# A fused attention and two-layer MoE kernel: pieces of the weights' conversion queued behind VectorE instructions of the steps

## The chip, the core and the metric

The kernel runs on one core of a Trainium2 chip, as one program. The metric is the device time of one execution in microseconds (us). The numbers of the profile come from one profiled execution, whose records start and end a little inside the device time.

## What is computed

Inputs are float32 queries, keys and values of 8 batches, 8 heads, 576 positions and a head size of 64, and two pairs of float64 weights, which the kernel reads as pairs of 32-bit words.

```python
k_p, v_p = k.reshape(B, H, 72, 8, D).mean(3), v.reshape(B, H, 72, 8, D).mean(3)
attn = softmax(q @ k_p.T / sqrt(D))            # B, H, 576, 72
x = (attn @ v_p) laid out as (4608, 512)
h = x @ w_in;   x = (h * cos(h)) @ w_out        # first layer, w_in 512x2048
h = x @ w_in2;  out = (h * clip(h + 3, 0, 6) / 6) @ w_out2
```

## The kernel before, in words

**Steps.** A layer is worked through in blocks of 512 tokens (9 of them) and in 16 chunks of 128 of the 2048 inner columns. One pair of a block and a chunk is a step. `gemm1` (L174) makes h of a step with 12 matmuls, `chain0` to `chain3` make the nonlinearity on ScalarE and VectorE, and `gemm2` (L236) multiplies with the second weight, again 12 matmuls, and comes two steps (`LAG`) later. Each product is of three matmuls: a value is split into a high part of reduced precision and the rest (xh and xl, gh and gl, wh and wl). There are 288 steps. Steps 0 to 58 are part A of the first layer, chunks 0 to 4 or 0 to 6 of each block, interleaved with the attention, since their weights fit beside it (`pool_a`, 7 chunks). Steps 59 to 143 are part B, the other chunks of each block, and add what part A left in `yp_d`. Steps 144 to 287 are the second layer.

**The chain of a step.** In the first layer: ScalarE t (L184) and g (L194), VectorE g (L195), ScalarE sine (L198), VectorE g times h (L208), ScalarE gh (L211), and then gl (L217) on VectorE or, in early steps, GpSimd. In the second layer: ScalarE relu (L186), VectorE L200, ScalarE gh, VectorE gl.

**The conversion.** Half a chunk's weights are one job, 64 jobs in all. A job reads 512 KB into `st` (two buffers, loaded by SyncE's queue), and has three pieces: first ScalarE's square e (L114) and VectorE's L115 and L119; second VectorE's L124 and L127; third ScalarE's wh (L132) and GpSimd's wl (L133). `w_fetch` requests the load for the job after the next one when a job is done. Tile a has two buffers.

**What sets the order.** The program is traced in the order of the code, and then a list scheduler puts the instructions of each engine into a fixed queue: among those that it holds ready, the one traced first goes first, and one that is ready sooner goes ahead of an earlier one that isn't. So a job traced late can be queued early. Engines run their queues in order. During the attention the jobs are traced at counted places (`WPRE`, `WAT`). After it, `need` traces whole jobs just ahead of the step that uses them. From the end of the attention the weights of chunks 7 to 15 go to `pool_b`, in the room that the attention leaves. The weights of the second layer take the same buffers chunk by chunk, as the first layer ends its use of them: chunks 0 to 6 in part B, chunks 7 to 15 in the last block of part B.

**Input blocks.** `fetch_x` loads four 128x512 tiles xr of a block with SyncE's queue (three buffers). `split_x` makes xh on ScalarE (L151) and xl on GpSimd (L152), with six buffers each: two of the next block's four pairs can be made while a block runs, the other two only when the block's last `gemm1` lets go of its first tiles.

The line numbers are those of the profile. In the changed program the lines from L615 on stand some 18 lines lower, and the lines named above keep their numbers.

Of the kernel before, what the change touches and what calls it, by code (L numbers as in the profile page):

```python
# [29 lines left out]
def tile_kernel(ctx, tc, q, k, v, wi1, wo1, wi2, wo2, ident_d, mask_d, out):  # L30
    nc = tc.nc
# [7 lines left out]
    NF = wo1.shape[0] // P  # L39
# [3 lines left out]
    LAG = 2  # L43
# [32 lines left out]
    pool_a = ctx.enter_context(tc.tile_pool(name="pool_a", bufs=NA))  # L76
# [12 lines left out]
    def fetch_weights(m, fc, half):  # L89
        st = stg.tile([P, 2 * HW], U32, tag="st", name="st", bufs=2)  # L90
        wi, wo = words[m]
        if half == 0:
            nc.sync.dma_start(
                out=st.rearrange("p (c j) -> p c j", j=2 * P),
                in_=wi[:, fc * 2 * P : (fc + 1) * 2 * P].rearrange("(c p) j -> p c j", p=P),
            )
        else:
            nc.sync.dma_start(out=st, in_=wo[fc * P : (fc + 1) * P, :])
        staged[m, fc, half] = st
# [57 lines left out]
    nc.vector.memset(bias_c[:, 1:2], math.pi / 2)  # L157
    nc.vector.memset(bias_c[:, 2:3], 3.0)

    hs, gs, gt, yps, yprev = {}, {}, {}, {}, {}  # L160

    ps_h2 = None

# [25 lines left out]
    def chain1(s):  # L189
        m = steps[s][0]  # L190
        g, t = gs[s]
        h = hs[s]
        if m == 0:
            nc.scalar.activation(out=g, in_=t, func=AF.Copy, bias=MAGIC, scale=1.0)  # L194
            nc.vector.scalar_tensor_tensor(  # L195
                out=g, in0=g, scalar=MAGIC, in1=t, op0=ALU.subtract, op1=ALU.subtract
            )
            nc.scalar.activation(out=g, in_=g, func=AF.Sin, scale=-TWO_PI)  # L198
        else:
            nc.vector.scalar_tensor_tensor(  # L200
                out=g, in0=g, scalar=6.0, in1=h, op0=ALU.min, op1=ALU.mult
            )

# [330 lines left out]
    for bl in range(NB):  # L534
        n = NAL[bl]
        steps += [(0, (0, bl), bl, fc, fc == 0, fc == n - 1) for fc in range(n)]
    SA = len(steps)
    for bl in range(NB):
        n = NAL[bl]
        steps += [(0, (1, bl), bl, fc, fc == n, fc == NF - 1) for fc in range(n, NF)]  # L540
    SB = len(steps)
# [22 lines left out]
    live = True  # L564

    wjobs = [(0, fc, hf, "a") for fc in range(NA) for hf in range(2)]
    fetched = 0
    converted = 0

    def w_fetch():  # L570
        nonlocal fetched
        if fetched < len(wjobs) and fetched < converted + 2:
            fetch_weights(*wjobs[fetched][:3])
            fetched += 1

    running = []
    whole = set()

    def w_ops(n):
        while running and n:  # L580
            running.pop(0)()
            n -= 1
            if not running:
                whole.add(wjobs[converted - 1][:3])
                w_fetch()

    def need(s):
        m, _, _, fc = steps[s][:4]
        while (m, fc, 1) not in whole:
            w_convert(pool_a if wjobs[converted][3] == "a" else pool_b)  # L590

    def w_convert(pool, n=3):
        nonlocal converted
        m, fc, hf, _ = wjobs[converted]
        converted += 1
        running.extend(convert_weights(m, fc, hf, pool))
        w_ops(n)

    w_fetch()
    w_fetch()  # L600
    npieces = 0
    while not started:
        next(att)
        npieces += 1
        while converted < len(WPRE) and WPRE[converted] <= npieces:
            w_convert(pool_a)
    for c in range(NC):
        fetch_x(0, (0, 0), 0, c)
    for c in range(NC):
        split_x((0, 0), c)  # L610

    pool_b = None
    T = len(steps)
    after = {}
    ypl = None  # L615
# [1 line left out]
    for slot in range(2 * (T + LAG) + 4):  # L617
        s, odd = divmod(slot, 2)
        for fn in after.pop(slot, ()):
            fn()  # L620
        if not odd and s < T:
            m, key, bl, fc, first, last = steps[s]
# [32 lines left out]
        if odd and s >= LAG and s - LAG < T:  # L655
            gemm2(s - LAG)
        while converted - len(WPRE) < len(WAT) and WAT[converted - len(WPRE)] <= slot:
            w_convert(pool_a)
        if live:
            key = steps[s][1]  # L660
            i = sum(1 for x in steps[:s] if x[1] == key)
# [5 lines left out]
            while live and npieces < goal:  # L667
                try:
# [3 lines left out]
                    live = False  # L672
                    actx.close()
                    ps_h2 = ctx.enter_context(tc.tile_pool(name="ps_h2", bufs=2, space=PSUM))
                    pool_b = ctx.enter_context(tc.tile_pool(name="pool_b", bufs=NF - NA))
# [54 lines left out]
```

## Time and profile before

| | before |
|---|---|
| median of 3 runs | 1856.01 us (1854.77 to 1856.22) |
| the profiled execution | 1853.73 us |
| its span | 1851.9 us |
| TensorE (PE) matmuls busy | 1763.0 us, 8016 instructions |
| VectorE (DVE) busy | 929.0 us |
| ScalarE (ACT) busy | 874.0 us |
| GpSimd (POOL) busy | 405.3 us |

The share of busy time is a mean over stages with different limits: the attention (to about 455 us), part B and the second layer. The views of the profile used below are the busy time of each engine by stretch, the waits by who waited for whom, the groups of instructions by line, and instructions in order of time. PEclk is the clock that TensorE was granted, as a share of 2.4 GHz.

### The profile page before, as it was taken

How to read it: one execution, taken by the hardware profiler on the slowest of the kernel's cores; microseconds unless marked ns; L12 is line 12 of the kernel's file. 1: busy time of each engine (PE TensorE's matmuls, PEld its weight loads, DVE VectorE, ACT ScalarE, POOL GpSimd, SP SyncE). 2: the span in 40 equal slices, each digit the busy share in tenths (PEclk: the TensorE clock that was granted, in tenths of full speed). 3: DMA queues.
4: the chain of work that ended last, by engine and by line, in shares of the span. 5: the costliest groups of instructions: out<-in, count | busy, mean ns of one | idle time of the engine just before them, and what ended most of it. 6: DMA issues, size and time to landing. Idle time of an engine off the chain costs nothing.

```text
span 1851.9 us, 21118 instructions
## 1 busy us (share of the span) xinstructions
PE 1763.0 (95%) x8016; PEld 1441.0 (78%) x8016; DVE 929.0 (50%) x1386; ACT 874.0 (47%) x1472; POOL 405.3 (22%) x302
## 2 busy tenths in 40 slices
PE   5689999999888999999999899999999999999999
PEld 4567777887666888888888678888888888888887
DVE  7999656655989464444444962222222222222222
ACT  3568677776666555555555533232323232322222
POOL 3765344322434111111112421010101010100000
PEclk8799999999999999999999999999999999999999
DMA  7656352323534022222222420010101010101000
GB/s 206 182 173 207 112 158 74 88 75 113 157 125 157 25 91 69 69 68 69 69 68 69 136 69 29 18 46 1 46 1 46 1 46 0 46 1 40 1 23 24
DMA packets 114630, 138.82 MB, mean 75 GB/s; under 512 B 44256, under 2 KB 68960, under 8 KB 114528
## 3 DMA queue, kind: packets, MB, share of 16 engines
q1 hardware_dynamic: 114528, 137.47, 24.2%
q8 instruction: 63, 1.03, 0.2%
q14 instruction: 39, 0.32, 0.1%
HBM read 99.69 MB, written 37.75 MB: 74 GB/s over the span
## 4 chain that ended last, share of the span: by engine, by line
PE 76%; DVE 13%; issue 4%; ACT 3%; DMA 2%; POOL 2%; SPq 0%; DVEq 0%; ACTq 0%; POOLq 0%
PE h L174 36%; PE y L236 36%; DVE a L119 2%; PE ap_ps L468 2%; DVE a L127 2%; PE ap_ps L392 1%; DVE a L115 1%; DVE a L124 1%; DVE g L195 1%; DVE raw L321 1%; DMA raw<-in_k_dram 1%; DVE gl L217 1%; POOL xl L152 1%; DMA xr<-x_d 1%; DVE sm L414 1%
## 5 line engine op out<-in xcount | busy, mean ns | idle before, releaser
L174 PE MATMUL h<-xl,wh 128*128 128x512 f32 x1152 | 453.7, 394 | 13.1 <-POOL xl L152 13.0
L174 PE MATMUL h<-xh,wh 128*128 128x512 f32 x1152 | 453.3, 394 | 1.3 <-ACT xh L151 1.3
L174 PE MATMUL h<-xh,wl 128*128 128x512 f32 x1152 | 450.4, 391 | 0.0
L152 POOL TENSOR_TENSOR xl<-xr,xh 128x512 fp32r<-128x512 f32 x108 | 151.3, 1420 | 932.3 <-ACT xh L151 931.4
L200 DVE SCALAR_TENSOR_TENSOR g<-g,h 128x512 f32<-128x512 f32 x144 | 99.2, 689 | 457.2 <-ACT g L186 457.2
L186 ACT ACTIVATE g<-h,bias_c 128x512 f32<-128x512 f32 x144 | 99.0, 687 | 424.6 <-PE h L174 424.2
L211 ACT ACTIVATE gh<-g 128x512 fp32r<-128x512 f32 x288 | 181.8, 631 | 180.0 <-DVE g L200 104.8
L174 PEld LDWEIGHTS h<-xl,wh 128*128 128x128 f32 x1152 | 217.1, 188 | 62.8 <-POOL xl L152 19.2
L217 DVE TENSOR_TENSOR gl<-g,gh 128x512 fp32r<-128x512 f32 x255 | 190.9, 749 | 146.8 <-ACT gh L211 139.3
L174 PEld LDWEIGHTS h<-xh,wh 128*128 128x128 f32 x1152 | 217.0, 188 | 46.6 <-ACT xh L151 2.1
L174 PEld LDWEIGHTS h<-xh,wl 128*128 128x128 f32 x1152 | 216.9, 188 | 44.3 <-issue 0.4
L236 PE MATMUL y<-gh,wh 128*128 128x512 f32 x576 | 231.8, 402 | 11.0 <-ACT gh L211 5.8
L236 PE MATMUL y<-gl,wh 128*128 128x512 f32 x576 | 230.6, 400 | 6.6 <-DVE gl L217 6.4
L236 PE MATMUL y<-gh,wl 128*128 128x512 f32 x576 | 229.0, 398 | 0.0
L236 PE MATMUL y<-wh,gh 128*128 128x512 f32 x576 | 224.2, 389 | 1.1 <-DVE yv L244 1.1
L236 PE MATMUL y<-wh,gl 128*128 128x512 f32 x576 | 224.1, 389 | 0.0
L236 PE MATMUL y<-wl,gh 128*128 128x512 f32 x576 | 224.1, 389 | 0.0
L195 DVE SCALAR_TENSOR_TENSOR g<-g,t 128x512 f32<-128x512 f32 x144 | 115.9, 805 | 146.8 <-ACT g L194 146.6
L236 PEld LDWEIGHTS y<-gh,wh 128*128 128x128 f32 x576 | 110.5, 192 | 37.7 <-ACT gh L211 7.7
L198 ACT ACTIVATE g<-g 128x512 f32<-128x512 f32 x144 | 90.9, 631 | 97.2 <-DVE g L195 96.9
L236 PEld LDWEIGHTS y<-gl,wh 128*128 128x128 f32 x576 | 110.6, 192 | 33.0 <-DVE gl L217 11.1
L184 ACT ACTIVATE t<-h 128x512 f32<-128x512 f32 x144 | 85.1, 591 | 105.6 <-PE h L174 105.4
(93 smaller groups left out, 2137.4 us busy)
## 6 DMA issues: line engine op xcount, KB each, us to landing
xr<-x_d SPq DMA_DIRECT2D x72, 256.0 KB, 2.9
st<-in_moe_w_in_dram SPq DMA_DIRECT2D x32, 512.0 KB, 3.8
st<-in_moe_w_out_dram SPq DMA_DIRECT2D x32, 512.0 KB, 3.3
yp_d<-ys SPq DMA_DIRECT2D x36, 256.0 KB, 2.4
yv<-yp_d SPq DMA_DIRECT2D x36, 256.0 KB, 3.5
xr<-y_d SPq DMA_DIRECT2D x36, 256.0 KB, 2.8
out_dram<-ys SPq DMA_DIRECT2D x36, 256.0 KB, 2.1
raw<-in_k_dram SPq DMA_DIRECT2D x8, 1024.0 KB, 5.7
```

The source lines that it names most:

```text
L119: nc.vector.scalar_tensor_tensor(out=a, in0=lo, scalar=29, in1=a, op0=ALU.logical_shift_right, op1=ALU.bitwise_or)
L127: nc.vector.scalar_tensor_tensor(out=w, in0=e, scalar=2.0**-30, in1=w, op0=ALU.is_ge, op1=ALU.mult)
L152: nc.gpsimd.tensor_tensor(out=xl, in0=t, in1=f(xh), op=ALU.subtract)
L174: nc.tensor.matmul(h, a[:, cs], z, start=(n == 0), stop=(n == 3 * NC - 1))
L184: nc.scalar.activation(out=t, in_=hs[s], func=AF.Copy, bias=0.25, scale=INV_2PI)
L186: nc.scalar.activation(out=g, in_=hs[s], func=AF.Relu, bias=bias_c[:, 2:3], scale=1.0)
L195: nc.vector.scalar_tensor_tensor(out=g, in0=g, scalar=MAGIC, in1=t, op0=ALU.subtract, op1=ALU.subtract)
L198: nc.scalar.activation(out=g, in_=g, func=AF.Sin, scale=-TWO_PI)
L200: nc.vector.scalar_tensor_tensor(out=g, in0=g, scalar=6.0, in1=h, op0=ALU.min, op1=ALU.mult)
L211: nc.scalar.activation(out=gh, in_=g, func=AF.Copy)
L217: eng.tensor_tensor(out=gl, in0=gs[s][0], in1=f(gh), op=ALU.subtract)
L236: nc.tensor.matmul(y[c], a, z, start=(first and n == 0), stop=(last and n == 2))
```

## The change

A step's first VectorE instruction that makes g (L195 or L200) is kept as `mark`. From the end of the attention on, `w_ahead` traces pieces of the jobs after every half of a step: for jobs of the first layer one piece per half step, for chunks 0 to 6 of the second layer one per step, for chunks 7 to 15 three per step. What a piece does on VectorE gets an edge behind a mark, of the step before in the first half of a step and of the step itself in the second. The edge fixes the order in VectorE's queue and waits for nothing. A job of the second layer isn't traced before the step at which its buffer is let go of. `need` is still there and ends what is not done in time. What the jobs compute is the same.

```diff
-            nc.vector.scalar_tensor_tensor(
+            mark[s] = nc.vector.scalar_tensor_tensor(
                 out=g, in0=g, scalar=MAGIC, in1=t, op0=ALU.subtract, op1=ALU.subtract
...
         while (m, fc, 1) not in whole:
-            w_convert(pool_a if wjobs[converted][3] == "a" else pool_b)
+            if running:
+                w_ops(len(running))
+            else:
+                w_convert()
...
+    def w_ahead(s, odd):
+        if not running:
+            if converted == len(wjobs):
+                return
+            m, fc, _, home = wjobs[converted]
+            if m == 1 and s < (SA + LAG if home == "a" else SB - NF + fc + LAG):
+                return
+            w_convert(0)
+        m, _, _, home = wjobs[converted - 1]
+        n = 1 + odd if m == 1 and home == "b" else 1 if m == 0 else odd
+        if n:
+            with tc.issue_after(mark[s - 1 + odd].ins):
+                w_ops(n)
...
+        if not live:
+            w_ahead(s, odd)
```

The built programs show how the queues come out. In the rows below a, e, st, wh and wl belong to the conversion, g, h, t, gh and gl to a step, xr, xh and xl to an input block.

VectorE, from the first conversion after the attention, before (L195 with g_4422 is step 41):

```order
L115 TENSOR_SCALAR a_5295<-st_5232 128x512
L119 SCALAR_TENSOR_TENSOR a_5295<-st_5232,a_5295 128x512
L115 TENSOR_SCALAR a_5306<-st_5243 128x512
L124 SCALAR_TENSOR_TENSOR a_5295<-st_5232,a_5295 128x512
L119 SCALAR_TENSOR_TENSOR a_5306<-st_5243,a_5306 128x512
L195 SCALAR_TENSOR_TENSOR g_4422<-g_4422,t_4423 128x512
L127 SCALAR_TENSOR_TENSOR a_5295<-e_5296,a_5295 128x512
L124 SCALAR_TENSOR_TENSOR a_5306<-st_5243,a_5306 128x512
L208 TENSOR_TENSOR g_4422<-h_4409,g_4422 128x512
L127 SCALAR_TENSOR_TENSOR a_5306<-e_5307,a_5306 128x512
L115 TENSOR_SCALAR a_5359<-st_5304 128x512
L217 TENSOR_TENSOR gl_4430<-g_4422,gh_4429 128x512
```

The same place in the changed program (g_4357 is step 40, g_4429 step 41):

```order
L195 SCALAR_TENSOR_TENSOR g_4357<-g_4357,t_4358 128x512
L115 TENSOR_SCALAR a_4411<-st_4389 128x512
L119 SCALAR_TENSOR_TENSOR a_4411<-st_4389,a_4411 128x512
L208 TENSOR_TENSOR g_4357<-h_4344,g_4357 128x512
L124 SCALAR_TENSOR_TENSOR a_4411<-st_4389,a_4411 128x512
L127 SCALAR_TENSOR_TENSOR a_4411<-e_4412,a_4411 128x512
L217 TENSOR_TENSOR gl_4365<-g_4357,gh_4364 128x512
L195 SCALAR_TENSOR_TENSOR g_4429<-g_4429,t_4430 128x512
L115 TENSOR_SCALAR a_4490<-st_4391 128x512
L119 SCALAR_TENSOR_TENSOR a_4490<-st_4391,a_4490 128x512
L208 TENSOR_TENSOR g_4429<-h_4416,g_4429 128x512
L217 TENSOR_TENSOR gl_4437<-g_4429,gh_4436 128x512
```

Before, all eight instructions of two jobs and the first of a third stand ahead of step 41's gl (the last row); now a step has two or four conversion instructions in its row, a pair at a time. Jobs 15 to 32, the first layer's, stand at steps 40 to 65 now, two jobs in three steps; before, jobs 17 to 44 stood at steps 40 to 59. Jobs 33 to 46 stand at steps 67 to 106 now, one in three steps.

GpSimd at the same place, before (xl_4558 and xl_4562 are the last two tiles of the block that starts at step 45):

```order
L133 TENSOR_TENSOR wl_5222<-a_5223,wh_5221 128x512
L133 TENSOR_TENSOR wl_5222<-a_5234,wh_5221 128x512
L133 TENSOR_TENSOR wl_5294<-a_5295,wh_5293 128x512
L133 TENSOR_TENSOR wl_5294<-a_5306,wh_5293 128x512
L133 TENSOR_TENSOR wl_5358<-a_5359,wh_5357 128x512
L133 TENSOR_TENSOR wl_5358<-a_5370,wh_5357 128x512
L152 TENSOR_TENSOR xl_4558<-xr_4437,xh_4557 128x512
L133 TENSOR_TENSOR wl_5418<-a_5419,wh_5417 128x512
L152 TENSOR_TENSOR xl_4562<-xr_4439,xh_4561 128x512
L152 TENSOR_TENSOR xl_4806<-xr_4725,xh_4805 128x512
L152 TENSOR_TENSOR xl_4822<-xr_4727,xh_4821 128x512
L133 TENSOR_TENSOR wl_5418<-a_5430,wh_5417 128x512
```

and in the changed program, from its first wl after the attention (there the two tiles are xl_4591 and xl_4595):

```order
L133 TENSOR_TENSOR wl_4410<-a_4411,wh_4409 128x512
L133 TENSOR_TENSOR wl_4410<-a_4490,wh_4409 128x512
L152 TENSOR_TENSOR xl_4591<-xr_4444,xh_4590 128x512
L152 TENSOR_TENSOR xl_4595<-xr_4446,xh_4594 128x512
L133 TENSOR_TENSOR wl_4554<-a_4555,wh_4553 128x512
L152 TENSOR_TENSOR xl_4887<-xr_4786,xh_4886 128x512
L152 TENSOR_TENSOR xl_4907<-xr_4788,xh_4906 128x512
L133 TENSOR_TENSOR wl_4554<-a_4638,wh_4553 128x512
L133 TENSOR_TENSOR wl_4710<-a_4711,wh_4709 128x512
L133 TENSOR_TENSOR wl_4710<-a_4794,wh_4709 128x512
L133 TENSOR_TENSOR wl_4854<-a_4855,wh_4853 128x512
L152 TENSOR_TENSOR xl_4940<-xr_4790,xh_4939 128x512
```

The two xl tiles stood behind six wl, with one more between them; now they stand behind two wl and next to each other.

VectorE near the end of the first layer, before (from step 138's L195 to step 139's):

```order
L195 SCALAR_TENSOR_TENSOR g_8634<-g_8634,t_8635 128x512
L119 SCALAR_TENSOR_TENSOR a_9334<-st_9287,a_9334 128x512
L124 SCALAR_TENSOR_TENSOR a_9334<-st_9287,a_9334 128x512
L208 TENSOR_TENSOR g_8634<-h_8621,g_8634 128x512
L127 SCALAR_TENSOR_TENSOR a_9334<-e_9335,a_9334 128x512
L115 TENSOR_SCALAR a_9379<-st_9332 128x512
L217 TENSOR_TENSOR gl_8642<-g_8634,gh_8641 128x512
L119 SCALAR_TENSOR_TENSOR a_9379<-st_9332,a_9379 128x512
L124 SCALAR_TENSOR_TENSOR a_9379<-st_9332,a_9379 128x512
L115 TENSOR_SCALAR a_9390<-st_9343 128x512
L195 SCALAR_TENSOR_TENSOR g_8670<-g_8670,t_8671 128x512
```

and in the changed program (the same two steps, g_8815 and g_8862):

```order
L195 SCALAR_TENSOR_TENSOR g_8815<-g_8815,t_8816 128x512
L124 SCALAR_TENSOR_TENSOR a_8826<-st_7583,a_8826 128x512
L115 TENSOR_SCALAR a_8883<-st_8800 128x512
L208 TENSOR_TENSOR g_8815<-h_8802,g_8815 128x512
L127 SCALAR_TENSOR_TENSOR a_8826<-e_8827,a_8826 128x512
L119 SCALAR_TENSOR_TENSOR a_8883<-st_8800,a_8883 128x512
L217 TENSOR_TENSOR gl_8823<-g_8815,gh_8822 128x512
L195 SCALAR_TENSOR_TENSOR g_8862<-g_8862,t_8863 128x512
```

Seven conversion instructions stood between two L195; now there are four. Before, jobs 49 to 64 stood at steps 137 to 146, sixteen jobs in ten steps; now jobs 47 to 64 stand at steps 136 to 153, one job per step.

VectorE in the attention, at step 8, as a difference (minus is before, plus is the changed program):

```order
-L115 TENSOR_SCALAR a<-st 128x512
-L416 RECIPROCAL sm<-sm 128x8
-L119 SCALAR_TENSOR_TENSOR a<-st,a 128x512
-L195 SCALAR_TENSOR_TENSOR g<-g,t 128x512
-L124 SCALAR_TENSOR_TENSOR a<-st,a 128x512
-L115 TENSOR_SCALAR a<-st 128x512
-L127 SCALAR_TENSOR_TENSOR a<-e,a 128x512
-L119 SCALAR_TENSOR_TENSOR a<-st,a 128x512
-L208 TENSOR_TENSOR g<-h,g 128x512
-L124 SCALAR_TENSOR_TENSOR a<-st,a 128x512
-L127 SCALAR_TENSOR_TENSOR a<-e,a 128x512
+L416 RECIPROCAL sm<-sm 128x8
```

The VectorE instructions of two jobs, which the scheduler had drawn forward by more than 30 steps, stand at steps 40 to 42 now; L195 and L208 come back as plus lines right behind these. With them two loads of st leave this place of SyncE's queue, and the order of matmuls of steps 9 to 15 shifts against that of the attention; ScalarE gets one more pair of table loads there, 54 in all after 52. From step 36 on the order on TensorE is the same in both programs.

## Rows read from the trace of the kernel before

**Rows 1.** The page's busy times, and its chain that ended last, by engine.

```profile
PE 1763.0 (95%) x8016; PEld 1441.0 (78%) x8016; DVE 929.0 (50%) x1386; ACT 874.0 (47%) x1472; POOL 405.3 (22%) x302
PE 76%; DVE 13%; issue 4%; ACT 3%; DMA 2%; POOL 2%; SPq 0%; DVEq 0%; ACTq 0%; POOLq 0%
```

**Rows 2.** Busy by stretch: from:to length, us (count) per engine, clock, DMA, GB/s.

```profile
455.00:600.00 145.00, 126.25 (x503) 96.76 (x502) 136.76 (x171) 89.43 (x159) 58.70 (x41) 0.95 0.46 145
600.00:1008.00 408.00, 408.00 (x1802) 337.84 (x1801) 187.54 (x260) 216.43 (x360) 70.09 (x52) 1.00 0.21 65
725.00:1000.00 275.00, 275.00 (x1215) 227.68 (x1215) 117.84 (x162) 142.65 (x236) 46.30 (x34) 1.00 0.20 61
1008.00:1075.00 67.00, 58.83 (x233) 45.79 (x232) 63.00 (x80) 36.97 (x64) 30.32 (x21) 0.92 0.46 145
1075.00:1830.00 755.00, 755.00 (x3332) 625.14 (x3331) 213.02 (x308) 215.37 (x332) 43.90 (x35) 1.00 0.07 24
```

**Rows 3.** The same view, the last slices of either slow stretch.

```profile
575.00:600.00 25.00, 20.27 (x71) 14.85 (x72) 24.25 (x28) 16.52 (x31) 12.57 (x8) 0.86 0.52 164
1050.00:1075.00 25.00, 18.59 (x66) 13.51 (x65) 24.76 (x28) 12.44 (x23) 16.49 (x11) 0.86 0.44 137
```

**Rows 4.** TensorE's waits, 455 to 600 us: total us, times, longest.

```profile
PE y L236 <- DVE gl L217: 5.4, 7, 1.4
PE y L236 <- ACT ys L252: 5.2, 4, 1.9
PE h L174 <- POOL xl L152: 4.8, 4, 2.4
```

**Rows 5.** VectorE by line, 455 to 600 us: xcount, us, mean ns, idle.

```profile
L119 DVE SCALAR_TENSOR_TENSOR a<-st,a 128x512 uint32<-128x512 uint32 x28 | 33.0, 1180 | 0.3
L124 DVE SCALAR_TENSOR_TENSOR a<-st,a 128x512 uint32<-128x512 uint32 x28 | 28.9, 1033 | 0.7
L127 DVE SCALAR_TENSOR_TENSOR a<-e,a 128x512 f32<-128x512 bf16 x28 | 22.5, 805 | 0.3
L115 DVE TENSOR_SCALAR a<-st 128x512 uint32<-128x512 uint32 x28 | 17.1, 612 | 2.4 <-POOL wl L133 2.4
```

**Rows 6.** In order of time: start us, us, engine, instruction, [idle before it].

```profile
476.63 1.27 POOL L152 TENSOR_TENSOR xl<-xr,xh 128x512 fp32r<-128x512 f32 x1 [2.42 <-ACT xh L151]
...
477.86 1.73 POOL L133 TENSOR_TENSOR wl<-a,wh 128x512 fp32r<-128x512 f32 x1
...
481.31 0.61 PE L174 MATMUL h<-xl,wh 128*128 128x512 f32 x1 [2.41 <-POOL xl L152]
...
489.45 1.36 POOL L133 TENSOR_TENSOR wl<-a,wh 128x512 fp32r<-128x512 f32 x1 [1.29 <-ACT wh L132]
...
489.68 1.68 DVE L119 SCALAR_TENSOR_TENSOR a<-st,a 128x512 uint32<-128x512 uint32 x1
```

**Rows 7.** Busy by stretch and VectorE's groups, 655 to 671 us, in part B.

```profile
655.00:671.00 16.00, 16.00 (x72) 13.26 (x71) 12.32 (x17) 9.35 (x16) 5.20 (x4) 1.00 0.54 179
...
L119 DVE SCALAR_TENSOR_TENSOR a<-st,a 128x512 uint32<-128x512 uint32 x3 | 3.2, 1053 | 0.0
...
L127 DVE SCALAR_TENSOR_TENSOR a<-e,a 128x512 f32<-128x512 bf16 x2 | 1.9, 972 | 0.0
```

**Rows 8.** In order of time there: first and last instruction of one step's chain.

```profile
655.66 0.60 ACT L184 ACTIVATE t<-h 128x512 f32<-128x512 f32 x1 [1.40 <-PE h L174]
...
662.39 0.69 DVE L217 TENSOR_TENSOR gl<-g,gh 128x512 fp32r<-128x512 f32 x1
```

**Rows 9.** The attention: by stretch, two jobs' first and last instruction, table loads.

```profile
150.00:250.00 100.00, 90.85 (x490) 72.96 (x489) 73.97 (x127) 73.94 (x131) 52.96 (x41) 1.00 0.51 156
...
170.36 0.41 DVE L115 TENSOR_SCALAR a<-st 128x512 uint32<-128x512 uint32 x1
...
176.88 1.34 DVE L127 SCALAR_TENSOR_TENSOR a<-e,a 128x512 f32<-128x512 bf16 x1
...
L198 ACT ACT_TABLE_LOAD x26 | 33.4, 1283 | 0.5
```

More of the change, by code (lines that the diff above doesn't have):

```diff
@@ L158, in tile_kernel @@
     nc.vector.memset(bias_c[:, 2:3], 3.0)
-    hs, gs, gt, yps, yprev = {}, {}, {}, {}, {}
+    hs, gs, gt, yps, yprev, mark = {}, {}, {}, {}, {}, {}
     ps_h2 = None
@@ L199, in chain1 @@
         else:
-            nc.vector.scalar_tensor_tensor(
+            mark[s] = nc.vector.scalar_tensor_tensor(
                 out=g, in0=g, scalar=6.0, in1=h, op0=ALU.min, op1=ALU.mult
@@ L589, in need, with w_convert @@
         while (m, fc, 1) not in whole:
-            w_convert(pool_a if wjobs[converted][3] == "a" else pool_b)
-    def w_convert(pool, n=3):
+            if running:
+                w_ops(len(running))
+            else:
+                w_convert()
+    def w_convert(n=3):
         nonlocal converted
-        m, fc, hf, _ = wjobs[converted]
+        m, fc, hf, home = wjobs[converted]
         converted += 1
+        pool = pool_a if home == "a" else pool_b
         running.extend(convert_weights(m, fc, hf, pool))
         w_ops(n)
+    def w_ahead(s, odd):
[11 more added lines that the diff above has]
+                w_ops(n)
+    pool_b = None
     w_fetch()
@@ L605, in tile_kernel @@
         while converted < len(WPRE) and WPRE[converted] <= npieces:
-            w_convert(pool_a)
+            w_convert()
     for c in range(NC):
@@ L610, in tile_kernel @@
         split_x((0, 0), c)
-    pool_b = None
     T = len(steps)
@@ L657, in tile_kernel @@
         while converted - len(WPRE) < len(WAT) and WAT[converted - len(WPRE)] <= slot:
-            w_convert(pool_a)
+            w_convert()
+        if not live:
+            w_ahead(s, odd)
         if live:
```

## The prediction

> **What bounds the kernel now.** I read the page's busy times and chain first. TensorE is busy for 95% of the span and holds 76% of the chain that ended last, VectorE 13% [rows 1]. That looks like a kernel with nothing left, so the next view is the busy time by stretch. From 1075 to 1830 us TensorE is busy without a break: 3332 matmuls in 755.00 us, 0.2266 us each; from 600 to 1008 us it is 1802 in 408.00 us, 0.2264 each [rows 2]. A step has 24 matmuls, so at this pace it lasts 5.43 us. Two stretches fall behind it. From 455 to 600 us there are 503 matmuls, worth 503 x 0.2265 = 113.9 us, in 145 us: 31.1 us lost. From 1008 to 1075 us there are 233, worth 52.8 us, in 67 us: 14.2 us lost. In both VectorE is busy 94% of the time (136.76 of 145, 63.00 of 67), elsewhere under half of it [rows 2]. These are the two stretches in which the scheduler packed the conversion. So there VectorE sets the pace, and TensorE elsewhere.
>
> How the loss comes about: TensorE stands idle for 145 - 126.25 = 18.8 us of the first stretch and 8.2 us of the second [rows 2]. It waits above all for gl of VectorE (5.4 us), for the output block's copy on ScalarE (5.2 us) and for xl of GpSimd (4.8 us) [rows 4]; all three stand behind conversion instructions, or behind work that does. The remaining 12.3 and 6.0 us are clock: the granted clock is 0.95 and 0.92 there and 0.86 in the last slice of each [rows 2, 3], a mix of the 2.4 and 1.2 GHz levels, where it is 1.00 in the stretches without idle time. So that part goes when the idle time goes.
>
> **The change part by part.**
>
> *The order itself.* No instruction is added but one pair of table loads; 64 jobs stay 64 jobs. In the first stretch VectorE did 28 jobs (28 of L119 [rows 5]) in 503 / 24 = 21.0 steps, 1.34 per step; near the second its queue has sixteen jobs at ten steps, 1.6 per step. In the changed program it is 0.67 per step (steps 40 to 65), 0.33 (67 to 106) and 1 (136 to 153).
>
> *Does VectorE then fit in a step?* Its own work in part B without a conversion is 117.84 us over 1215 / 24 = 50.6 steps, 2.33 us per step (725 to 1000 us [rows 2]). What a job adds is bounded from both sides. In the packed stretch VectorE was busy 136.76 / 21.0 = 6.53 us per step, so a job added (6.53 - 2.33) / 1.34 = 3.1 us. From 655 to 671 us, 2.94 steps, it was busy 12.32 / 2.94 = 4.18 us per step with 3 of L119 and 2 of L127 [rows 7], about 2.5 jobs or 0.85 per step: 2.2 us a job. So at 0.67 jobs a step needs 3.8 to 4.4 us, at one job 4.5 to 5.5 us, of 5.43. In the second layer VectorE's own work is 213.02 us over 138.8 steps, 1.53 us [rows 2], and a job per step makes 3.7 to 4.6 us. I take the lower price, since it stands where jobs were spread at nearly one per step, and there TensorE was busy 16.00 of 16.00 us [rows 7]. That row is the nearest to what the change makes everywhere.
>
> *The latency that hides it.* The pairs now stand inside a step's chain, between L195, L208 and gl. The cover is the lag: gl of a step is wanted four blocks of twelve matmuls after the end of its `gemm1`, 10.9 us. In the loaded stretch a chain ran from 655.66 to 663.08 us, 7.4 us [rows 8], so 3.5 us of cover are left there.
>
> *What goes.* With VectorE below a step's length the three waits of the first stretch go, and with them the clock's part: -31.1 us. In the second: -14.2 us. Together -45.3 us. The GpSimd queue is part of it: at 476.63 us it makes one xl, then a wl of 1.73 us stands ahead of the next xl, and TensorE waits 2.41 us [rows 6]; in the changed queue these two xl stand together. SyncE's loads of st wait for a job's reads as before, and the loads of xr behind them now wait for one or two jobs at 0.67 per step; the first xl that depends on them is wanted some seven steps later, so I count nothing for it; without that cover it would be the 2.41 us again.
>
> *What is late next.* At block boundaries and at the change of layer, ScalarE's wh waits for L127 and stands ahead of xh, and some wl still stand between xl tiles. Five boundaries (steps 45, 52, 59, 70, 144) lie in the loaded steps. The bounds are 0, as in rows 7, and 5 x 1.6 = 8 us with two thirds of the longest xl wait at each. I take 2 us.
>
> *The attention.* Two jobs leave VectorE at 170.36 to 178.2 us [rows 9], in a stretch in which TensorE lacks 9.15 us of 100. Their eight instructions took about 5 us of VectorE's queue, so a gain of up to 5 us can't be excluded. Against it stand two table loads of 1.28 us on ScalarE [rows 9] and another interleaving of steps 9 to 15, which could lose as much as this stretch already lacks, 9 us. Nothing in the rows favours a sign; I take 0. From step 36 on TensorE's order is the same, and what shifts here shifts the end.
>
> *Sum.* 1853.7 - 45.3 + 2 = 1810.4 us for an execution like the profiled one. That one was 2.3 us under the median of the runs shown (1856.0), so the time is 1812.7 us.
>
> *A rule against it.* L119 took 1.68 us at 489.68 us, when a wl ran on GpSimd from 489.45 to 490.81 us: it ended 0.55 us after the wl [rows 6], while the mean of L119 is 1.18 us [rows 5]. So a GpSimd instruction seems to hold VectorE up. The Trainium skill says why (SBUF — State Buffer, section "SBUF: two separate sides"): the two engines share a port pair under an exclusive lock, and the loser "fully blocks". By that rule spreading removes no collision: each of the wl still stops VectorE once, and the gain would have to come from idle time alone. The trace agrees as far as L119 shows it. What it would make of the time is the first rival.
>
> **The rivals.**
>
> *VectorE is still too slow at one job per step.* In steps 136 to 143 a step has 1 wl and, per 11 steps, 4 xl and 2 ys, 1.55 GpSimd instructions of 58.70 / 41 = 1.43 us [rows 2], 2.2 us. If all of it is added to the 4.5 us, a step needs 6.7 us, 1.3 more than 5.43; over eight steps 10 us, less the 3.5 us of cover: 7 us, and with the clock's part (6.0 of 14.2 in that stretch) 11 to 12 us. 1812.7 - 2 + 11 = about 1822 us. (This is the lock of the Trainium skill's SBUF page, taken in full.) For it: the upper price, 5.5 us, is already above a step. Against it: rows 7 hold 5.20 us of GpSimd in 2.94 steps, 1.77 us per step, and its collisions are in their 4.18 us.
>
> *The attention's new order costs more than it frees.* 6 to 9 us: 1819 to 1822 us. For it: this stretch has little room, and queues are tied to each other there. Against it: what leaves is VectorE work at a place where VectorE was behind.
>
> *Slower than before: the chain outgrows the lag.* The in-order VectorE would then set a step in all loaded steps, not only in the packed ones. The changed program has 26 steps at 0.67, 40 at 0.33 and 18 at one job, and to eat 45.3 us the 44 steps at 0.67 and at one would each have to last 1.03 us longer, 6.46 us. With a lag of two steps that takes a chain of 12.9 us instead of 7.4 [rows 8], or 6.46 us of VectorE per step instead of 5.5 at most. Beyond that point the time would pass 1856, say 1862 us. Nothing in the rows comes near it.
>
> *The change doesn't do what it says:* the jobs would still bunch, since the edges only fix an order. The built queue speaks against it: four conversion instructions per step where seven stood. 1856 us.
>
> **How the numbers follow.** The forecast, 1812.7 us, has 0.70; its own range is 1807 to 1819 (0 to 8 us of late work). VectorE too slow at one job, about 1822: 0.13. The attention's loss, 1819 to 1822 and beyond: 0.08. A gain in the attention beyond the forecast's range, 1803 to 1807: 0.04. Slower, 1862: 0.03. No effect: 0.02. The range of 1805 to 1823 us holds the forecast, most of the first two rivals and half of the gain, about 0.84, and leaves out the rest. Within 0.2% (3.7 us, about what a measurement of this kernel can tell from no change) lies only the last case, 0.02; slower is 0.03; faster is the rest, 0.95.
>
> **What would show it.** In the profile after, TensorE should be busy without a break and at clock 1.00 from the end of the attention to the end, with 110 matmuls in each 25 us; VectorE between 60% and 85% busy in part B's first 27 steps and at the change of layer; no wait for gl there. The first rival would show waits of TensorE for gl or gh around step 140 and a clock below 1.00; the second a later end of the attention than about 455 us. I am wrong if idle time stays in the first stretch although VectorE is no longer busy there: then the bound was a transfer or a buffer and not VectorE's queue.

## The result and the profile after

The changed kernel takes 1807.72 us (median of 4 runs, 1807.15 to 1808.24), beside 1855.39 us for the kernel before on the same chip (4 runs, 1854.64 to 1856.22): a ratio of 0.9743, 95% interval 0.9726 to 0.976, or 47.7 us. The profiled execution took 1808.24 us with a span of 1806.5 us. That is inside the forecast's range of 1805 to 1823, 5.0 us under the forecast itself.

The page of the changed kernel, busy times and the chain by engine, which answer to [rows 1]:

```profile
PE 1748.0 (97%) x8016; PEld 1438.5 (80%) x8016; DVE 892.1 (49%) x1386; ACT 876.9 (49%) x1474; POOL 402.9 (22%) x302
PE 86%; DVE 7%; ACT 3%; issue 2%; POOL 1%; DMA 1%; SPq 0%; DVEq 0%; ACTq 0%; POOLq 0%
```

VectorE's part of the chain has fallen from 13% to 7%. Its 1386 instructions are as many as before, but they are busy 36.9 us less.

Busy time by stretch, in the changed kernel (columns as in [rows 2]):

```profile
455.00:600.00 145.00, 145.00 (x641) 119.79 (x640) 102.77 (x149) 93.79 (x165) 42.50 (x31) 1.00 0.35 113
600.00:1008.00 408.00, 408.00 (x1802) 337.84 (x1801) 226.15 (x321) 230.44 (x387) 95.44 (x67) 1.00 0.27 87
985.00:1015.00 30.00, 30.00 (x134) 24.83 (x133) 23.74 (x36) 19.82 (x34) 13.19 (x8) 1.00 0.32 99
1025.00:1050.00 25.00, 23.91 (x104) 19.17 (x103) 19.55 (x32) 12.22 (x21) 9.09 (x7) 1.00 0.48 146
1075.00:1800.00 725.00, 725.00 (x3200) 600.55 (x3199) 194.48 (x282) 202.91 (x312) 39.03 (x31) 1.00 0.07 22
```

Where 503 matmuls ran in 145 us before there are 641, TensorE has no idle time, the clock is 1.00 instead of 0.95, and VectorE is busy 102.77 us instead of 136.76. From 600 to 1008 us TensorE does the same 1802 matmuls as before while VectorE does 38.6 us more: the work went where there was room. One slice is short, at 1025 us, and all waits of TensorE from 450 us to the end are one row (where [rows 4] has three of about 5 us):

```profile
PE y L236 <- DVE yv L244: 1.1, 1, 1.1
```

It is read best in order of time. VectorE, then GpSimd, then TensorE, of the changed kernel at 1025 us (start us, us, engine, instruction):

```profile
1025.15 1.77 DVE L124 SCALAR_TENSOR_TENSOR a<-st,a 128x512 uint32<-128x512 uint32 x1
1026.84 0.68 DVE L244 TENSOR_TENSOR yv<-y,yv 128x512 f32<-128x512 f32 x1
```

```profile
1025.08 2.98 POOL L254 TENSOR_TENSOR ys<-ys,yv 128x512 f32<-128x512 f32 x2 [0.32 <-ACT ys L252]
```

```profile
1027.58 0.50 PE L236 MATMUL y<-wh,gh 128*128 128x512 f32 x1 [1.07 <-DVE yv L244]
```

Two additions of GpSimd start at 1025.08 us, a conversion's L124 beside them takes 1.77 us, and the addition yv, which reads an output block and so frees it for TensorE, stands behind it in VectorE's queue. This is at the change of layer, one of the five boundaries for which the prediction had put 2 us.

VectorE by line, 455 to 600 us, in the changed kernel (instructions, busy us, mean ns, idle before), which answers to [rows 5]:

```profile
L195 DVE SCALAR_TENSOR_TENSOR g<-g,t 128x512 f32<-128x512 f32 x27 | 20.5, 758 | 26.6 <-ACT g L194 26.6
...
L208 DVE TENSOR_TENSOR g<-h,g 128x512 f32<-128x512 f32 x27 | 18.5, 684 | 0.0
L127 DVE SCALAR_TENSOR_TENSOR a<-e,a 128x512 f32<-128x512 bf16 x17 | 13.7, 807 | 0.6
L119 DVE SCALAR_TENSOR_TENSOR a<-st,a 128x512 uint32<-128x512 uint32 x18 | 13.4, 747 | 0.6
L124 DVE SCALAR_TENSOR_TENSOR a<-st,a 128x512 uint32<-128x512 uint32 x17 | 13.1, 769 | 0.0
L115 DVE TENSOR_SCALAR a<-st 128x512 uint32<-128x512 uint32 x18 | 9.7, 541 | 0.0
```

L119 fell from 1180 to 747 ns and L124 from 1033 to 769. A job's four means add up to 2.86 us, where they were 3.63 before.

### The profile page after: what moved, and what is told of

It is laid out like the page before. It is cut to its first block, busy times and chain, and to the rows that moved or that the text cites. A ratio compares the mean times of both kernels' runs of the same rounds, so it can differ in the third digit from the quotient of the medians.

```text
span 1806.5 us, 21050 instructions
## 1 busy us (share of the span) xinstructions
PE 1748.0 (97%) x8016; PEld 1438.5 (80%) x8016; DVE 892.1 (49%) x1386; ACT 876.9 (49%) x1474; POOL 402.9 (22%) x302
## 4 chain that ended last, share of the span: by engine, by line
PE 86%; DVE 7%; ACT 3%; issue 2%; POOL 1%; DMA 1%; SPq 0%; DVEq 0%; ACTq 0%; POOLq 0%
PE h L174 41%; PE y L236 40%; PE ap_ps L468 2%; PE ap_ps L392 2%; DVE raw L321 1%; DVE g L195 1%; POOL xl L152 1%; DVE sm L414 1%; DMA xr<-x_d 1%; DVE a L127 0%; PE ap_ps L438 0%; DVE e L403 0%; DVE ptl L422 0%; DVE a L124 0%; DVE a L115 0%
## 5 line engine op out<-in xcount | busy, mean ns | idle before, releaser
L200 DVE SCALAR_TENSOR_TENSOR g<-g,h 128x512 f32<-128x512 f32 x144 | 99.2, 689 | 455.0 <-ACT g L186 455.0
L217 DVE TENSOR_TENSOR gl<-g,gh 128x512 fp32r<-128x512 f32 x255 | 190.2, 746 | 159.4 <-ACT gh L211 156.1
L174 PEld LDWEIGHTS h<-xh,wh 128*128 128x128 f32 x1152 | 217.1, 189 | 44.3 <-issue 0.6
L236 PE MATMUL y<-gh,wh 128*128 128x512 f32 x576 | 227.6, 395 | 0.0
L236 PE MATMUL y<-gl,wh 128*128 128x512 f32 x576 | 226.5, 393 | 0.0
L195 DVE SCALAR_TENSOR_TENSOR g<-g,t 128x512 f32<-128x512 f32 x144 | 112.1, 779 | 144.2 <-ACT g L194 144.1
L133 POOL TENSOR_TENSOR wl<-a,wh 128x512 fp32r<-128x512 f32 x64 | 87.3, 1364 | 282.9 <-ACT wh L132 282.8
L236 PEld LDWEIGHTS y<-wh,gh 128*128 128x128 f32 x576 | 108.1, 188 | 24.1 <-DVE yv L244 1.9
```

The source lines that it names most:

```text
L133: nc.gpsimd.tensor_tensor(out=wl, in0=w, in1=f(wh), op=ALU.subtract)
L174: nc.tensor.matmul(h, a[:, cs], z, start=(n == 0), stop=(n == 3 * NC - 1))
L195: mark[s] = nc.vector.scalar_tensor_tensor(out=g, in0=g, scalar=MAGIC, in1=t, op0=ALU.subtract, op1=ALU.subtract)
L200: mark[s] = nc.vector.scalar_tensor_tensor(out=g, in0=g, scalar=6.0, in1=h, op0=ALU.min, op1=ALU.mult)
L217: eng.tensor_tensor(out=gl, in0=gs[s][0], in1=f(gh), op=ALU.subtract)
L236: nc.tensor.matmul(y[c], a, z, start=(first and n == 0), stop=(last and n == 2))
```

## The experiments

All are edits of the changed kernel. Times are medians; the changed kernel stands at 1807.7 us, and at 1807.2 us in the last experiment. The ratios are to the kernel before, which was run beside each set of experiments and stands at 1855.1 to 1855.8 us there: between sets, a difference of about 1 us tells nothing.

**Is it the edges?** The pieces are traced at the same places, but without an edge behind a mark.

```diff
-            with tc.issue_after(mark[s - 1 + odd].ins):
-                w_ops(n)
+            w_ops(n)
```

> The pieces are traced at the changed kernel's places, but without the edge behind a mark. The scheduler then draws all of them forward again: the built queues of all five engines are those of the kernel before, but for the names of buffers. Theory (the order in VectorE's queue is all of the change): 1855.4 us as before, within 1 us. Rival (the place in the traced program, and the loads requested there, matter by themselves): under 1850 us.

1854.04 us, ratio 0.9994 (0.9984 to 1.0003). The scheduler drew the pieces forward to where they stood before, and the time is the kernel before's. The edge is the whole change; the place in the code alone changes nothing that these runs can tell. A slice of the attention and the first stretch in this kernel, and that slice in the kernel before:

```profile
170.00:200.00 30.00, 24.78 (x127) 18.95 (x126) 23.04 (x42) 17.93 (x33) 20.12 (x15) 0.94 0.51 151
455.00:600.00 145.00, 126.11 (x503) 96.59 (x502) 136.26 (x171) 88.95 (x159) 59.75 (x41) 0.95 0.45 143
```

```profile
170.00:200.00 30.00, 24.67 (x134) 18.93 (x134) 23.46 (x43) 19.40 (x36) 20.85 (x16) 1.00 0.51 154
```

The first stretch is that of [rows 2]. The attention is not: the granted clock fell in this execution, and 127 matmuls ran where there had been 134. The part on the prediction comes back to this.

**Are the two packed stretches two separate losses?** First the last 18 jobs, those of chunks 7 to 15 of the second layer, go back to their old places.

```diff
             m, fc, _, home = wjobs[converted]
+            if m == 1 and home == "b":
+                return
```

> The changed kernel without the spreading of the last 18 jobs (chunks 7 to 15 of the second layer), which fall back to their old places, 16 of them at steps 137 to 146. Theory (VectorE's packed queue sets the pace there): the 14.2 us of the stretch at the change of layer come back, less the 1.1 us that TensorE still waits there now: about 1807.7 + 13 = 1821 us, with the granted clock below 1.00 near 1050 us. Rival (one stretch feeds the other, or the attention made the gain): 1808 to 1812 us.

1820.28 us, ratio 0.981 (0.9796 to 0.9825): 12.6 us lost, as expected. The second stretch is back. Busy time of two slices in this kernel:

```profile
1000.00:1025.00 25.00, 20.26 (x72) 14.77 (x71) 24.89 (x31) 14.17 (x25) 12.75 (x9) 0.86 0.45 141
1025.00:1050.00 25.00, 20.88 (x87) 15.71 (x87) 24.56 (x33) 12.35 (x21) 12.21 (x8) 1.00 0.47 154
```

The reverse was meant to spread these 18 jobs alone.

```diff
             m, fc, _, home = wjobs[converted]
+            if m == 0 or home == "a":
+                return
```

> Only the last 18 jobs are spread; all others stand where they stood before, two of them in the attention and 30 in the 20 steps behind it. Theory: the 31.1 us of the first stretch come back and those of the second do not, 1807.7 + 31 + about 1 of the attention = 1840 us. Rival (the gain is of the second stretch or of the attention): under 1825 us.

1859.08 us, ratio 1.002 (1.0011 to 1.0029), a miss by 19 us. The edit did something else. `w_ahead` looks only at the next job in the list; jobs 33 to 46 stood ahead of the 18 until `need` traced them, and the 18 came at steps 148 to 158, in 10.5 steps. Busy time and TensorE's waits (1050 to 1150 us) show the packed stretch that this made:

```profile
1075.00:1100.00 25.00, 24.15 (x105) 19.36 (x104) 21.81 (x29) 11.89 (x20) 8.19 (x6) 1.00 0.40 125
1100.00:1125.00 25.00, 19.56 (x75) 14.72 (x74) 23.71 (x32) 11.45 (x19) 8.81 (x7) 0.93 0.40 128
```

```profile
PE h L174 <- ACT wh L132: 7.2, 5, 2.5
PE h L174 <- POOL wl L133: 4.5, 6, 1.1
```

Now TensorE waits for the weights themselves: later but packed is no better. Since this left open whether the two losses add, the experiment was made again with jobs 17 to 46 at the old places and the 18 at steps 136 to 153, as in the changed kernel.

```diff
-            if m == 1 and s < (SA + LAG if home == "a" else SB - NF + fc + LAG):
-                return
+            if home == "a" or m == 0:
+                if m == 0 or s < 136:
+                    return
+                while wjobs[converted][3] == "a":
+                    w_convert()
+                m, fc, _, home = wjobs[converted]
+            if s < SB - NF + fc + LAG:
+                return
```

> Only the last 18 jobs (chunks 7 to 15 of the second layer) are spread, one per step over steps 136 to 153, as in the changed kernel; jobs 17 to 46 stand packed at steps 40 to 72, as in the kernel before, and nothing stands packed later. Theory (the two losses are separate and add): the first stretch stays at about 31 us, the second is gone: the changed kernel's 1807.7 plus 31 plus the attention's 1.5 = about 1840 us (1837 to 1843), all idle time between 455 and 600 us. Rival (the losses are one: packing left anywhere breaks the pace, as e2 seemed to say): 1852 to 1859 us.

1842.56 us, ratio 0.9926 (0.9914 to 0.9939), 35.4 us above the changed kernel on the same chip. The first stretch is as in [rows 2], and the change of layer as in the changed kernel:

```profile
455.00:600.00 145.00, 127.13 (x504) 97.68 (x503) 135.57 (x171) 89.10 (x159) 59.79 (x41) 0.94 0.45 140
...
1050.00:1075.00 25.00, 23.91 (x104) 19.15 (x103) 20.61 (x31) 12.20 (x22) 10.19 (x8) 1.00 0.51 163
```

35.4 + 12.6 = 48.0 us, and the change gave 47.7. But the 35.4 is not the first stretch alone, since the two early jobs are back in the attention too. The stretches themselves can be read from the traces, because from step 36 on TensorE's order is the same and the same matmuls can be compared. From the 2001st to the 2601st the changed kernel gains 31.3 us on the kernel before and 30.7 on this one; from the 4501st to the 4651st it gains 13.0 us on the kernel before and 13.0 on the one without the late spreading. So the two losses are separate and add up.

**Does the rate of the jobs decide, or only that they are in order?** The first layer's 18 jobs, still even and behind marks, at 1.38 per step (steps 40 to 52).

```diff
         if not live:
             w_ahead(s, odd)
+            if wjobs[converted - 1][0] == 0:
+                w_ahead(s, odd)
```

> The 18 jobs of the first layer are spread with edges as in the changed kernel, but at four pieces a step, 1.38 jobs per step at steps 40 to 52, which is the packed stretch's mean rate (1.34). If the rate on VectorE is the limit, each of the 13 steps lasts the 6.92 us of the packed stretch: 13 x 1.48 = 19 us, less 3.5 us of cover: about 1807.7 + 16 = 1823 us. If it is the order (a packed queue makes VectorE and GpSimd collide and puts xl and gl behind conversions), VectorE needs 2.33 + 1.38 x 2.28 = 5.5 us of 5.43 at the price a job has in the changed kernel's trace: 0 to 3 us, 1808 to 1811 us.

1823.19 us, ratio 0.9828 (0.9812 to 0.9844), what the rate gives. Two slices, and VectorE's L119 from 455 to 525 us:

```profile
475.00:500.00 25.00, 20.63 (x81) 16.17 (x82) 23.12 (x33) 16.43 (x30) 9.48 (x8) 0.93 0.56 188
500.00:525.00 25.00, 22.31 (x89) 16.79 (x88) 23.14 (x29) 14.83 (x27) 11.05 (x8) 0.93 0.30 96
```

```profile
L119 DVE SCALAR_TENSOR_TENSOR a<-st,a 128x512 uint32<-128x512 uint32 x13 | 15.9, 1219 | 0.2
```

VectorE is packed again (23.1 of 25 us), L119 costs again what it cost before, and the clock falls with the idle time. That the loss is what the rate gives doesn't yet show that VectorE's busy time is the limit: the next run loses time with VectorE far from full. Then the same 18 jobs at one per step (steps 40 to 57).

```diff
-        n = 1 + odd if m == 1 and home == "b" else 1 if m == 0 else odd
+        n = 1 + odd if m == 1 and home == "b" else 2 if m == 0 else odd
```

> The first layer's 18 jobs stand at one job per step (steps 40 to 57) instead of two in three steps; everything else as in the changed kernel. If a step's own loop through ScalarE and VectorE (5.24 us with one job in the first layer) is the limit, it is still under TensorE's 5.43 us and the time rises by 0 to 3 us: 1808 to 1811 us. If the busy time of VectorE counts with collisions at the packed price (2.33 + 3.1 = 5.4 us a step), it is at the edge and 3 to 8 us are lost: 1811 to 1816 us.

1817.21 us, ratio 0.9793 (0.9779 to 0.9806), 10.1 us lost: more than both expected. Busy time by stretch, VectorE's waits and its L195 (450 to 560 us) in this kernel:

```profile
475.00:575.00 100.00, 93.11 (x396) 73.16 (x396) 78.89 (x108) 64.93 (x117) 33.45 (x24) 1.00 0.40 129
```

```profile
DVE g L195 <- ACT g L194: 19.0, 15, 2.1
```

```profile
L195 DVE SCALAR_TENSOR_TENSOR g<-g,t 128x512 f32<-128x512 f32 x17 | 18.0, 1060 | 19.0 <-ACT g L194 19.0
```

396 matmuls are 16.5 steps, 6.06 us each, yet VectorE is busy only 4.78 us of them. It waits for ScalarE's g, so the limit is neither engine's busy time; what fits is the loop through both queues. The changed kernel holds one job per step around 990 us without loss. There VectorE runs, in order of time:

```profile
989.29 0.69 DVE L195 SCALAR_TENSOR_TENSOR g<-g,t 128x512 f32<-128x512 f32 x1 [1.20 <-ACT g L194]
...
990.84 0.69 DVE L208 TENSOR_TENSOR g<-h,g 128x512 f32<-128x512 f32 x1
991.44 0.68 DVE L127 SCALAR_TENSOR_TENSOR a<-e,a 128x512 f32<-128x512 bf16 x1
...
994.53 0.69 DVE L195 SCALAR_TENSOR_TENSOR g<-g,t 128x512 f32<-128x512 f32 x1 [1.20 <-ACT g L194]
```

and ScalarE beside it:

```profile
991.56 0.63 ACT L211 ACTIVATE gh<-g 128x512 fp32r<-128x512 f32 x1 [0.91 <-DVE g L208]
992.16 0.63 ACT L132 ACTIVATE wh<-a 128x512 fp32r<-128x512 f32 x1
...
993.87 0.63 ACT L194 ACTIVATE g<-t 128x512 f32<-128x512 f32 x1
```

From L195 over L208, gh, wh, e, t and g to the next L195 are 5.24 us, just under the step's 5.43. At one job per step in the first stretch, VectorE, ScalarE and GpSimd at 502 us:

```profile
502.73 1.37 DVE L195 SCALAR_TENSOR_TENSOR g<-g,t 128x512 f32<-128x512 f32 x1 [0.62 <-ACT g L194]
...
505.08 0.68 DVE L208 TENSOR_TENSOR g<-h,g 128x512 f32<-128x512 f32 x1
505.68 0.68 DVE L124 SCALAR_TENSOR_TENSOR a<-st,a 128x512 uint32<-128x512 uint32 x1
506.40 0.69 DVE L127 SCALAR_TENSOR_TENSOR a<-e,a 128x512 f32<-128x512 bf16 x1
...
509.35 0.69 DVE L195 SCALAR_TENSOR_TENSOR g<-g,t 128x512 f32<-128x512 f32 x1 [1.66 <-ACT g L194]
```

```profile
505.80 0.63 ACT L211 ACTIVATE gh<-g 128x512 fp32r<-128x512 f32 x1 [1.03 <-DVE g L208]
507.12 0.63 ACT L132 ACTIVATE wh<-a 128x512 fp32r<-128x512 f32 x1 [0.69 <-DVE a L127]
...
508.68 0.63 ACT L194 ACTIVATE g<-t 128x512 f32<-128x512 f32 x1
```

```profile
502.25 1.30 POOL L133 TENSOR_TENSOR wl<-a,wh 128x512 fp32r<-128x512 f32 x1 [4.63 <-ACT wh L132]
```

This round lasts 6.62 us. L127 stands one conversion instruction later, wh waits 0.69 us for it ahead of the next step's t and g, and wl meets L195 (1.37 us; its mean is 1060 ns, 758 in the changed kernel). These two, 0.69 and 0.68 us, on top of 5.24 are this round's length. That the order within the job makes the difference is read from these two stretches; no run changed it alone. My expectation failed because it took the loop from a place where the pieces pair differently.

**Is the cutting into pieces needed, or only the mean rate?** The same rates, but each job's four VectorE instructions behind one mark.

```diff
-        n = 1 + odd if m == 1 and home == "b" else 1 if m == 0 else odd
+        n = 3 if m == 1 and home == "b" and odd else 3 if m == 0 and (2 * s + odd) % 3 == 0 else 3 if m == 1 and home == "a" and odd and s % 3 == 0 else 0
```

> Same mean rates as the changed kernel (0.67, 0.33 and 1 job per step), but a job is not cut in three: all four VectorE instructions of a job are queued behind one mark. Theory (the mean rate and the lag's cover decide): 3.5 us of cover swallow four instructions in a row, 1807 to 1810 us. Rival (the even cut is what matters, since a job in one go holds up the chain of a step): VectorE's work of one job, about 2.5 us, late in every step with a job; past the cover about 1 us in each of 18 steps at one job per step: 1820 us or more.

1813.64 us, ratio 0.978 (0.9766 to 0.9793): 5.9 us lost, between the two. TensorE's waits, 450 to 1100 us:

```profile
PE y L236 <- ACT ys L252: 3.2, 3, 1.4
PE y L236 <- DVE yv L244: 1.5, 1, 1.5
PE y L236 <- DVE gl L217: 1.1, 2, 0.7
```

The rate is worth most of the gain, the cutting about an eighth of it.

**Do GpSimd's instructions hold VectorE up?** GpSimd makes wl of the last 50 jobs twice (lines from L133 on move by two).

```diff
             nc.gpsimd.tensor_tensor(out=wl, in0=w, in1=f(wh), op=ALU.subtract)
+            if pool_b is not None:
+                nc.gpsimd.tensor_tensor(out=wl, in0=w, in1=f(wh), op=ALU.subtract)
```

> GpSimd makes wl of the last 50 jobs twice, the second time over the first. If a GpSimd instruction stops VectorE for its length, each adds up to 1.4 us to VectorE: 2 to 3 us per step in all at one job per step, 8 steps of the first layer at 5.24 + 1.4 = 6.6 us, 9 us less 3.5 of cover, and with the clock 6 to 10 us: 1814 to 1818 us. If the second one finds room beside VectorE's idle time: 1808 to 1810 us.

1825.19 us, ratio 0.9839 (0.9825 to 0.9852): 17.5 us lost, more than expected. TensorE's longest wait (450 to 1100 us), and the step's first VectorE instruction (455 to 600 us):

```profile
PE h L176 <- POOL xl L154: 7.8, 5, 2.6
```

```profile
L197 DVE SCALAR_TENSOR_TENSOR g<-g,t 128x512 f32<-128x512 f32 x25 | 28.8, 1150 | 25.0 <-ACT g L196 25.0
```

Both are there. VectorE's busy time is 924.9 us, 32.8 above the changed kernel's, 0.66 us for each wl added. By line, behind 455 us, 17.4 us of it fell on the instruction that makes g (in the stretch shown 1150 ns against 758) and 12.6 us on L124. But TensorE waits most for xl, which stands behind the second wl in GpSimd's own queue. So the run doesn't price the collisions alone.

**What did the attention bring?** Jobs 15 and 16 go without edges, and so to their old places at steps 7 and 8.

```diff
-            with tc.issue_after(mark[s - 1 + odd].ins):
+            if converted <= 2 * NA + 2:
                 w_ops(n)
+            else:
+                with tc.issue_after(mark[s - 1 + odd].ins):
+                    w_ops(n)
```

> The changed kernel without edges for the first two jobs (15 and 16), which the scheduler draws into the attention again, at steps 7 and 8. This measures the attention's part by itself: the attention ended 1.1 us sooner in the changed kernel's trace (448.65 against 449.78 us), after a start that was 1.1 us later, so 1 to 2.5 us come back: 1809 to 1810 us. If the attention has no part: 1807.7 us.

1809.22 us, ratio 0.9754 (0.974 to 0.9767): 1.5 us, as expected, though the intervals of the two ratios overlap and the two were not run side by side. Busy time from 150 to 250 us, first in the changed kernel and then in this one (before: 90.85, [rows 9]):

```profile
150.00:250.00 100.00, 93.94 (x503) 75.83 (x503) 67.98 (x122) 77.89 (x134) 51.98 (x42) 0.98 0.48 147
```

```profile
150.00:250.00 100.00, 90.88 (x489) 72.95 (x489) 73.91 (x127) 73.89 (x131) 52.89 (x41) 1.00 0.51 156
```

**Is the last stall all that is left behind the attention?** The last 18 jobs start at two in three steps up to step 143 and go on at one per step, to step 156.

```diff
-        n = 1 + odd if m == 1 and home == "b" else 1 if m == 0 else odd
+        n = (1 + odd if s >= SB else 1) if m == 1 and home == "b" else 1 if m == 0 else odd
```

> The last 18 jobs start at two pieces per step (0.67 jobs) to step 143 and go on with three from step 144, so that they end at step 156 instead of 153. Theory (one job per step in the first layer is at VectorE's and ScalarE's limit, 5.24 us around the loop): the last wait of TensorE behind the attention, 1.1 us for the output block's addition near 1027 us, goes: 1806.5 us. If it only moves: 1807.7 us.

1805.17 us, ratio 0.9734 (0.9721 to 0.9748). TensorE has no wait behind 450 us any more. It was run again beside the changed kernel on one chip.

> The changed kernel with the last 18 jobs at two in three steps up to step 143 and one per step from 144 on, beside the changed kernel on the same chip. If the last stall of 1.1 to 1.4 us at 1027 us is all there is to gain: 1.0 to 2.5 us under the changed kernel of this call. If the difference between calls was the chip's: equal within 0.7 us.

> The changed kernel unaltered, to be compared with the three kernels beside it on the same chip: 1807.7 us again, within 1 us.

1805.12 us (1804.4 to 1806.76), ratio 0.9728 (0.9715 to 0.9742), beside 1807.16 us (1807.05 to 1807.41), ratio 0.9738 (0.9724 to 0.9751). The runs don't overlap, though the intervals of the ratios do: 2.0 us. In both traces of this version 1.6 us lie around the wait, from the 4501st to the 4651st matmul, so the wait of 1.1 us costs somewhat more than its idle time; the rest arose before the late jobs begin, where the two kernels are the same. This is the fastest version here; what is left for the steps would have to come out of TensorE's own work.

## Why the prediction was right

- **The bound and its cure.** TensorE was to run without a break where VectorE's queue was no longer packed. It does: no gl wait, clock 1.00, 641 matmuls in 145 us (110 in 25 us were named); VectorE is busy 71% from 455 to 600 us and 79% at 985 us, inside the 60% to 85% named. Repacking either stretch brought its loss back. But ScalarE's wh and GpSimd's wl move with VectorE's pieces, and [rows 4] has waits for all three engines. No run moved one engine's part alone, so how much of the loss each queue made is not shown.
- **-45.3 us.** The first stretch was put at 31.1. Between the same matmuls it is 31.3 us shorter than in the kernel before, 30.9 than in the one without the edge, 30.7 than in the one with only the late jobs spread. The second was put at 14.2; it is 13.0 us shorter, and a wait of 1.1 us is left there. Together 45.4: this term was right.
- **The clock's part** came back with the idle time, and the clock fell again in the kernels that packed the queue again (0.86 and 0.93 in the slices shown). But the prediction put all of the remaining 12.3 and 6.0 us to the clock, and that split was wrong. The granted clock of 0.95 over 145 us and 0.92 over 67 us [rows 2] is worth about 7 and 5 us. The rest comes without any fall of the clock: at one job per step 396 matmuls kept TensorE busy for 93.11 us at clock 1.00, 3.4 us more than at 0.2265 us each, so a break costs more than its idle time. The sum didn't need the split; the price of the first rival did (6.0 of 14.2).
- **VectorE per step.** At 0.67 jobs it is 102.77 / (641 / 24) = 3.85 us, in the predicted 3.8 to 4.4. At one job it is 23.74 / (134 / 24) = 4.25 us, under the lower end of 4.5 to 5.5. I took the lower price of 2.2 us a job; measured are 2.3 and 1.9.
- **Late work, +2 us.** One wait of 1.1 us, at one of the five boundaries named; it needed the yv addition and a collision, which I had not named. The two stretches with it give 44.3 us where I had 43.3.
- **The attention, 0.** This term was too small. By medians the two jobs are worth 1.5 us. In the traces of the five kernels that have them at the old place, the 2001st matmul starts later than in the changed kernel by 1.1 us (before), 0.9 (the two early jobs), 2.8 (no edge), 2.9 (late jobs spread, first try) and 4.1 (second try). All this is inside the bounds (a gain of 5, a loss of 9). In the first two the granted clock is 1.00 from 170 to 200 us, in the other three 0.94. VectorE was busy 73.97 of 100 us there [rows 9], so the prediction's "elsewhere under half" doesn't hold for the attention.
- **From the profiled execution to the median.** Between the two profiled executions the gain is 1853.73 - 1808.24 = 45.5 us: 31.3, 13.0 and the attention's 1.1. Between the medians it is 47.7, where I had 43.3. I added 2.3 us to both kernels alike, as if the distance belonged to the device; the profiled execution after lies 0.5 above its median. So of the forecast's 5.0 us too much, 1.0 are the late work, 1.1 the attention and 2.8 this distance, all on the same side. Nor do the packed stretches vary: in the four traces that have the first it takes the same time within 0.6 us (503 or 504 matmuls in 145 us). What differs between these traces is the attention, where the profiled execution of the kernel before had no fall of the clock from 170 to 200 us and the one without the edge, with the same order and 1.2 us longer in all, had one. What makes the clock fall there in one execution and not in the other is not shown.
- **The first rival** has fallen in this kernel: 4.25 us at one job, no wait for gl or gh. But it was nearer than its 0.13 said, and by another mechanism: the loop through ScalarE and VectorE has 5.24 us there against 5.43, and at one job per step in the first stretch it was over. I looked at one engine's busy time and at the latency of one chain; the period of the loop, which sets the pace when both queues run in order, was missing.
- **The rule against it.** VectorE's busy time fell by 36.9 us with the same instructions and with the same 64 wl beside them. So spreading does remove collisions, contrary to what I drew from the rule. By the Trainium skill (SBUF — State Buffer, section "SBUF: two separate sides") the loser of the shared port is blocked fully; the 1.77 us of L124 beside GpSimd's additions agree with that, but the rule doesn't say how often the two meet. How often can be counted in the traces, behind 455 us, for VectorE's lines L115, L119, L124, L127, L195 and L217. Before, 93 of these instructions took over a quarter longer than usual, after 56, of 146 GpSimd instructions in either kernel. Every one of them began while a GpSimd instruction ran, and ended 0.55 us after it (L115: 0.28). Those that began beside one and didn't grow (2 before, 31 after) found at most 0.31 us of it left. Of the conversion's four instructions 55 were long before and 24 after: this is what spreading took away.

The other rivals fell plainly: the attention lost nothing, no chain outgrew the lag, and the jobs do not bunch.

## What to carry to other kernels

An engine that is busy half of the span can still be the bound where its in-order queue is packed: look for the stretches where it is nearly always busy (94% here), and price them by the bound engine's work missing there, idle time and clock together. Spread such work at a rate that fits a step and cut it finely, with the queue's order fixed by an edge, since code placed elsewhere is drawn back by a scheduler that works by readiness. Before raising the rate, add up the loop through all in-order queues of a step, not one engine's busy time.

## What had not been expected of the hardware

- The same 1386 VectorE instructions cost 929.0 us packed and 892.1 us spread; in the first stretch a job's four took 3.63 and 2.86 us.
- L208 never grew: 684 ns in the mean, while L195, L119, L124 and L127 stand at 747 to 807 in the same stretch. It alone of these reads a PSUM tile (h). Behind 455 us it began beside a GpSimd instruction 18 times before and 13 times after, and its longest took 0.69 us. This agrees with the Trainium skill (SBUF — State Buffer, section "SBUF: two separate sides"), which names VectorE instructions with two SBUF inputs, or in a 2-port mode, as those that take the shared port. L115, with one SBUF input, grew too (8 of 48 before); whether it runs in such a mode no run shows.
- A collision falls on what stands in VectorE's queue at that moment. With wl doubled, the step's first instruction went from 758 to 1150 ns in the first stretch; at 1025 us of the changed kernel it was L124, and TensorE waited 1.1 us. What a collision by itself costs TensorE no run shows.
- Between 0.67 and one job per step in the first stretch the time rises by 10.1 us with VectorE busy only 79%: the limit was met well below a full engine.
